# Attention, two mixtures of experts, one core: the second expert of the first mixture joins the block-by-block part

## The chip, the cores and the metric

One core of one Trainium2 chip runs the whole program. The metric is device time in microseconds (us). TensorE is PE in the profile, VectorE DVE, ScalarE ACT, GpSimd POOL, and SyncE SP; SP issues nearly all the transfers. PEld is TensorE's loading of weights.

## The reference

```
q, k, v: 2 batches x 8 heads x 768 tokens x 64
scores = q k^T / 8 - slope(h) * distance; kept: keys 0..7 and the last 96 keys
a = softmax(scores);  x = a v, as 1536 tokens x 512
mixture 1 (4 experts, all of them for every token):
    y = sum over e of p[:, e] * (relu(x @ w1[e]) @ w2[e]),   w1: 512 x 1024, w2: 1024 x 512
mixture 2 (8 experts, 192 tokens each, chosen by a greedy ranking of y @ w_gate):
    out[tokens of e] = relu(y[tokens of e] @ v1[e]) @ v2[e]
```

## The kernel before

**Numbers in two halves.** Each float32 operand of a matmul is scaled by a power of two and split into two float16 halves, hi and lo, and each product is three matmuls (hi hi, hi lo, lo hi). A weight matrix is fetched in two raw halves of 1 MB (`w_load`, L372); `w_norm` takes its sum of squares on ACT (L402) and turns it into a scale; then hi is made on ACT, POOL or DVE (`w_hi`, `scaled_on`, L540 to L544) and lo on DVE (`w_lows`, L473).

**Jobs.** The eight weight matrices of the first mixture are jobs 0 to 7, two for each expert. Job k's halves are `wl0.k` and `wl1.k` in the order below.

**First part (`phase1`).** Tokens come in 12 blocks j of 128. For each block the attention is done (load, scale, split, transposes by DMA, `qk`, `max` L706, `exp` L715, `ph` and `pl` that split the probabilities, `PT`, `pv`, `x`, `xT`: L770 issues the transpose of the finished block), and expert 0 follows behind: `g` (first layer, 12 matmuls of 128 columns per step, L834), `relu`, `hhi`, `hlo`, `y` (second layer, 3 matmuls of 512 columns per step, L845), `add`. Jobs 0 to 3 are fetched and split in between. The program order of all that is written out by hand in `ORDER1`, a list of names with a block number behind the point and an engine behind the slash; where no engine is named, the table `ENGINE` gives it. `AFTER` and the `after=` lists only check the order. Each engine runs its own instructions in this order.

**Second part (in `build`).** Expert 1 goes over the 12 blocks in three groups of four: 96 first-layer matmuls of 512 columns for each group, then 96 second-layer matmuls of 512. Meanwhile `pump` fetches and splits jobs 4, 5 and 6 (L402, L445, L447, L454).

**Third part (`phase3`)** runs experts 2 and 3 in pairs of blocks with the ranking of tokens behind; then `route`, in which the first weights of the second mixture are fetched into five raw buffers; then the second mixture, whose weights go through nine raw buffers.

The rule by which the second part groups its work:

```
jobs = [(e, j) for e in range(1, last - 1) for j in range(0, NB, 4)]
for e, j0 in jobs:
    ...
    for f in range(8):
        ps, st = s.g1(Ws[e], j0, j0 + 4, f, 1)
        ...
        s.hidden(ps, hh[:, f:f + 1], hl[:, f:f + 1])
        s.pump(1)
```

Of the kernel before, what the change touches and what calls it, by code (L numbers as in the profile page):

```python
# [42 lines left out]

ORDER1 = """
    load sq1 sq0 sq2 wl0 run wl1 route total scale wsq0 hi1/V load.1 hi0/A wsq1 lo1 lo0 hi2 sq1.1 lo2 wsum wsc gate0
    whi5 sq0.1 whi1/A whi3/V sq2.1 gate1 whi2/V wlo5 gate2 T0 T1 whi4/A run.1 load.2 total.1 wlo3 whi7/A swap tiles
# [2 lines left out]
    consts swap.1 keys.1/A max3 hi2.2 exp3 wsq0.1 lo2.1 pl0/V kglob.1 lo1.2 hi0.2 pl1/V qk0.1 ph2 load.3 sq1.3 lo0.2
    max0.1 exp0.1 PT0 wlo6 qk1.1 max1.1 pl2 qk2.1 ph3 pl3 PT1 bias1.1 max2.1 qk3.1 sq0.3 max3.1 pv lo2.2 wsq1.1 x  # L50
    ph0.1 pl0.1 wsum.1 sq2.3 T1.2 norm exp1.1 exp2.1 wsc.1 keys.2/G run.3 ph1.1/A both ph2.1/A total.3 T0.2 bias0.2
    whi1.1 rscale scale.3 xhi/V kglob.2 values.1/G load.4 exp3.1 xlo sq1.4 swap.2 xT pl1.1 wlo1.1 PT0.1 hi2.3/V hi1.3
    qk0.2 max0.2 lo1.3 pl2.1 ph3.1/A whi5.1/A pl3.1 qk1.2 sq0.4 lo2.3 wlo4 whi2.1 hi0.3/A vglob.1 g00 pe0 sq2.4
    bias1.2/A exp0.2 max1.2 g01 whi4.1 lo0.3 g02 g03 PT1.1 g10 T1.3 run.4 ph0.2 total.4 T0.3 wlo2.1 g11 qk2.2 pv.1
    scale.4 whi7.1 max2.2 qk3.2 load.5 x.1 swap.3 exp1.2 exp2.2 hi1.4 hi0.4 relu0 keys.3 bias0.3 pl0.2/V max3.2 norm.1
    g12 ph1.2/A ph2.2/V hhi0/A rscale.1 g13 xhi.1 exp3.2 sq1.5 whi3.1 lo0.4 kglob.3 xlo.1 pl2.2 whi0.1 ph3.2 wlo5.1
    sq0.5 lo1.4 T0.4 pl1.2/V qk0.3 xT.1 pl3.2 qk1.3 sq2.5 max0.3 max1.3 relu1 T1.4 qk2.3 values.2 qk3.3 hi2.4/A g00.1
    g01.1 g02.1 wlo0.1 vglob.2 bias1.3/A wlo4.1 PT0.2 keys.4 hhi1/A PT1.2 exp0.3 bias0.4 exp1.3 g03.1 whi6.1 ph0.3/A
    g10.1 run.5 hlo0 swap.4 max2.3 total.5 scale.5 y00 g11.1 y01 hi1.5 pv.2 g12.1 pl0.3/V ph1.3/A hi0.5 hlo1/V lo2.4
    kglob.4 lo0.5 pl1.3/V relu0.1 wl0.2 exp2.3 y02 x.2 qk0.4 g13.1 max3.3 norm.2 bias1.4 ph2.3/V wlo3.1 rscale.2  # L60
    exp3.3 load.6 xhi.2 PT0.3 sq1.6 hi2.5/V max0.4 xlo.2 qk1.4 ph3.3 lo1.5 wlo6.1 y03 T0.5 xT.2 exp0.4 sq0.6 pl2.3
    sq2.6 y04 max1.4 y05 qk2.4 pl3.3 T1.5 max2.4 qk3.4 values.3/G exp1.4 ph0.4 y06 exp2.4 run.6 keys.5 total.6 vglob.3
    wlo7.1 max3.4 kglob.5 g00.2 bias0.5 g01.2 scale.6 y07 tiles.1 relu1.1/V ph1.4 pl0.4/V pl1.4 g02.2 hi1.6 hhi0.1/A
    swap.5 g03.2 pe0.1 exp3.4 PT1.3 hlo0.1 qk0.5 lo2.5 pv.3 g10.2 hi0.6/A x.3 g11.2 ph2.4/A pl2.4 g12.2 load.7 max0.5
    y00.1 lo0.6 ph3.4/V sq1.7 PT0.4 bias1.5 norm.3 T0.6 rscale.3 qk1.5 pl3.4/V bias0.6 xhi.3/G hhi1.1 exp0.5 max1.5
    hlo1.1 PT1.4 sq0.7 values.4/A sq2.7 g13.2 qk2.5 ph0.5 xlo.3 add0 vglob.4 max2.5 y01.1 lo1.6 y02.1 hi2.6/V run.7
    pe0.2 xT.3 y03.1 y04.1 pl0.5 qk3.5 y05.1 exp1.5 relu0.2/V y06.1 ph1.5 exp2.5 lo2.6 max3.5 swap.6 pv.4 T1.6 y07.1
    ph2.5/A g00.3 total.7 g01.3 x.4 g02.3 pl1.5 relu1.2 scale.7 tiles.2 exp3.5 ph3.5/A hhi0.2 hi1.7/V bias1.6 qk0.6
    pl2.5 g03.3 norm.4 hi0.7/A pl3.5 PT0.5 qk1.6 hlo0.2 rscale.4 g10.3 max0.6 load.8 xhi.4/V hi2.7 g11.3 g12.3 g13.3
    values.5/A y00.2 sq1.8 lo0.7 qk2.6 hhi1.2/A xlo.4 PT1.5 lo1.7 exp0.6 y01.2 relu0.3/V y02.2 sq0.8 max1.6 pe0.3  # L70
    y03.2 T0.7 bias0.7 hlo1.2 ph0.6 y04.2 xT.4 T1.7 sq2.8 y05.2 qk3.6 vglob.5 y06.2 exp1.6 pv.5 y07.2 ph1.6 tiles.3
    max2.6 exp2.6 run.8 lo2.7 keys.7/G relu1.3/V pl0.6/V hhi0.3 load.9 hlo0.3 g00.4 add0.1/V kglob.7 g01.4 g02.4 g03.4
    total.8 g10.4 y00.3 swap.7 hhi1.3/G relu0.4 hlo1.3 g11.4 max3.6 x.5 exp3.6 y01.3 norm.5 ph2.6/V y02.3 pl2.6
    ph3.6/A sq1.9 scale.8 hi1.8 g12.4 qk0.7 y03.3 sq0.9 hi0.8/V qk1.7 pl1.6 y04.3 pl3.6/V lo0.8 rscale.5 xhi.5 bias1.7
    max0.7 g13.4 sq2.9 xlo.5 wl1.2 PT0.6 bias0.8 hi2.8/V max1.7 lo1.8 qk2.7 PT1.6 pe0.4 y05.3 T0.8 xT.5 y06.3 exp0.7
    y07.3 tiles.4 ph0.7 exp1.7 hhi0.4/G qk3.7 hlo0.4 max2.7 pv.6 T1.8 add0.3/V exp2.7 ph1.7 swap.8 add0.2 relu1.4
    lo2.8 y00.4 load.10 max3.7 y01.4 x.6 ph2.7 y02.4 keys.8/A g00.5 g01.5 run.9 exp3.7 y03.4 pl2.7/V total.9 kglob.8
    ph3.7/A g02.5 pl0.7 scale.9 qk0.8 g03.5 max0.8 norm.6 qk1.8 pl1.7 hhi1.4/A rscale.6 sq1.10 PT0.7 bias1.8 pl3.7
    exp0.8 g10.5 hlo1.4 g11.5 hi1.9 values.7 hi0.9/V pe0.5 g12.5 ph0.8 y04.4 lo0.9 qk2.8 g13.5 vglob.7 bias0.9/A
    max1.8 y05.4 sq0.10 y06.4 lo1.9 xhi.6/V relu0.5/V hi2.9/A qk3.8 PT1.7 xlo.6 pl0.8 y07.4 tiles.5 sq2.10 T0.9 exp1.8  # L80
    hhi0.5/G hlo0.5/V pv.7 relu1.5 T1.9 y00.5 keys.9/A max2.8 y01.5 ph1.8 xT.6 exp2.8 run.10 y02.5 hhi1.5/G lo2.9
    hlo1.5 pl1.8 max3.8 y03.5 exp3.8 swap.9 x.7 norm.7 load.11 total.10 y04.5 PT0.8 y05.5 g00.6 ph2.8 ph3.8/A kglob.9
    pl2.8 scale.10 rscale.7 g01.6 y06.5 xhi.7/G qk0.9 pl3.8/V hi1.10/A g02.6 g03.6 max0.9 sq1.11 xlo.7 qk1.9 hi0.10/A
    y07.5 sq0.11 exp0.9 PT1.8 relu0.6/V max1.9 g10.6 tiles.6 hhi0.6/A bias1.9 pe0.6 qk2.9 exp1.9 values.8 xT.7
    bias0.10 lo0.10 g11.6 g12.6 g13.6 hlo0.6 add0.4 ph0.9/V T0.10 vglob.8 qk3.9 sq2.11 max2.9 lo1.10 y00.6 y01.6 pv.8
    g00.7 T1.10 relu1.6 g01.7 exp2.9 run.11 pl0.9 max3.9 hhi1.6/A g02.7 g03.7 swap.10 values.9 keys.10 x.8 exp3.9
    ph1.9 y02.6 pl1.9 ph2.9 kglob.10 total.11 g10.7 hlo1.6 PT0.9 g11.7 g12.7 scale.11 ph3.9/A norm.8 qk0.10 qk1.10
    y03.6 hi2.10/A rscale.8 pl2.9 g13.7 max0.10 pl3.9 qk2.10 hi1.11/A PT1.9 xhi.8 relu0.7 exp0.10 xlo.8 xT.8 bias1.10
    ph0.10 y04.6 y05.6 max1.10 vglob.9 max2.10 y06.6 hi0.11/V hi2.11/V exp1.10 y07.6 pv.9 exp2.10 ph1.10 lo0.11 qk3.10
    tiles.7 hhi0.7 T0.11 max3.10 g00.8 g01.8 relu1.7 lo2.10 lo2.11 lo1.11 pl0.10 ph2.10/A hlo0.7/V pe0.7 values.10/G  # L90
    g02.8 exp3.10 g03.8 hhi1.7 add0.6 g10.8 pl2.10 x.9 add0.5/V T1.11 ph3.10/V g11.8 relu0.8/V g12.8 y00.7 y01.7
    pl1.10 y02.7 hlo1.7 swap.11 close0 keys.11 bias0.11/A y03.7 kglob.11 gate3 y04.7 wsq0.2 y05.7 pe0.8 y06.7 norm.9
    y07.7 qk0.11 rscale.9 PT0.10 wsq1.2 qk1.11 g13.8 max0.11 tiles.8 hhi0.8/A pl3.10 relu1.8/V hlo0.8 max1.11 y00.8
    y01.8 vglob.10 qk2.11 PT1.10 xhi.9 xlo.9 y02.8 bias1.11 y03.8 pv.10 exp0.11 qk3.11 hhi1.8 max2.11 wsum.2 hlo1.8/V
    ph0.11/A exp1.11 y04.8 exp2.11 pl0.11/V ph1.11 max3.11 xT.9 y05.8 ph2.11/V pl1.11/V y06.8 pl2.11/V y07.8 g00.9
    g01.9 x.10 exp3.11 ph3.11/A pl3.11/V norm.10 tiles.9 add0.7/V g02.9 g03.9 g10.9 g11.9 g12.9 relu0.9/V PT0.11
    rscale.10 hhi0.9/G hlo0.9/V pe0.9 g13.9 xhi.10/G y00.9 relu1.9/V values.11/A xlo.10 vglob.11 hhi1.9 wsc.2 y01.9
# [1748 lines left out]
```

## Time and profile before

| | |
|---|---|
| median of 3 runs | 895.22 us (891.95 to 895.56) |
| the profiled execution | 895.84 us, of which the span of its instructions is 894.1 us |
| busy over the span | PE 755.8 us (85%), DVE 645.1 (72%), PEld 544.6 (61%), ACT 528.1 (59%), POOL 334.4 (37%) |
| mean granted TensorE clock | 0.962 of 2.4 GHz |

PE's busy time counts each matmul to its modelled end, and matmuls overlap, so what a stretch of matmuls costs is read from start to start. DVE's instructions overlap a little as well: the sum of their durations is larger than the time in which DVE was busy.

### The profile page before, as it was taken

To read this page: it belongs to the slowest core of one execution; us is meant where nothing else is said; L and a number is where in the kernel's file an instruction comes from. 1 tells how busy PE (TensorE), PEld (TensorE's weight loads), DVE (VectorE), ACT (ScalarE), POOL (GpSimd) and SP (SyncE) were. 2 spreads that over 40 slices of the span, in tenths; PEclk is the share of its full clock that TensorE was granted. 3 is DMA by queue.
4 is the path that set the end of the run, shared out by engine and by line. 5 is a ranking of instruction groups with operands and counts; after the bars stand their busy time and mean duration, and the time that the engine had idled before them with its cause. 6 is when DMAs were issued, how large, how long until landed. Compare 5 with 4: busy or idle time off the path is not lost.

```text
span 894.1 us, 19304 instructions
## 1 busy us (share of the span) xinstructions
PE 755.8 (85%) x7539; PEld 544.6 (61%) x7539; DVE 645.1 (72%) x1710; ACT 528.1 (59%) x1046; POOL 334.4 (37%) x403
## 2 busy tenths in 40 slices
...
GB/s 232 217 177 184 178 188 212 151 112 139 154 142 0 108 81 1 95 31 89 1 26 12 14 25 14 36 2 1 59 213 84 131 139 347 247 277 321 193 34 39
DMA packets 196860, 105.20 MB, mean 118 GB/s; under 512 B 167585, under 2 KB 167585, under 8 KB 196769
## 3 DMA queue, kind: packets, MB, share of 16 engines
...
## 4 chain that ended last, share of the span: by engine, by line
PE 41%; DVE 25%; issue 12%; DMA 9%; ACT 7%; POOL 4%; SPq 1%; POOLq 0%; DVEq 0%; ACTq 0%
PE pH L834 16%; PE pY L845 14%; DVE C L967 3%; PE pR L834 2%; PE pY L1012 2%; ACT junk L402 2%; DVE jk L970 2%; DMA xt<-xs 2%; DVE t L706 2%; DMA xk<-in_k_dram 2%; PE pH L1255 2%; DMA xg<-g 2%; DVE w L473 1%; PE pR L1275 1%; POOL out_dram L1291 1%
## 5 line engine op out<-in xcount | busy, mean ns | idle before, releaser
L834 PE MATMUL pH<-xT,w 128*128 128x128 f16 (+2 forms) x2304 | 238.7, 263 | 10.7 <-DMA xT<-xs 9.2
L834 PEld LDWEIGHTS <-w 128*128 128x128 f16 x2592 | 209.0, 100 | 61.8 <-DMA xT<-xs 7.1
L845 PE MATMUL pY<-w,hh 128*128 128x512 f16 x544 | 162.3, 380 | 3.7 <-DVE y L544 1.3
L808 ACT ACTIVATE H<-pH 128x512 f32<-128x512 f32 (+1 forms) x94 | 52.8, 564 | 100.6 <-PE pH L834 75.8
L845 PE MATMUL pY<-w,hl 128*128 128x512 f16 x272 | 103.4, 380 | 4.2 <-POOL hl L1383 3.1
L980 ACT ACTIVATE Cj<-C 128x128 bf16<-128x128 bf16 (+11 forms) x88 | 75.3, 856 | 43.1 <-DVE C L967 42.1
L542 POOL TENSOR_SCALAR hh<-H 128x512 f16<-128x512 f32 x55 | 36.6, 665 | 134.3 <-ACT H L808 123.8
L845 PEld LDWEIGHTS <-hh 128*128 128x128 f16 x544 | 49.9, 98 | 52.9 <-issue 2.6
L1255 PEld LDWEIGHTS <-w 128*128 128x128 f16 x768 | 65.5, 100 | 23.4 <-DMA xg<-g 18.5
L432 DVE SCALAR_TENSOR_TENSOR w<-raw,wsr,w 128x1024 f16<-128x1024 f32 x52 | 65.2, 1278 | 6.3 <-ACT w L540 6.3
L1275 PE MATMUL pR<-hh,w 128*128 128x192 f16 x512 | 67.1, 249 | 0.0
L1255 PE MATMUL pH<-xg,w 128*128 128x192 f16 x528 | 49.8, 254 | 20.2 <-DMA xg<-g 18.3
L803 DVE TENSOR_TENSOR hl<-H,hh 128x384 f16<-128x384 f32 (+1 forms) x56 | 34.6, 617 | 44.2 <-POOL hh L542 43.1
L967 DVE TENSOR_SCALAR C<-LR,Lg 128x1024 bf16<-128x1024 f32 (+7 forms) x88 | 64.1, 729 | 3.1 <-PE pw L986 1.7
L1275 PEld LDWEIGHTS <-w 128*128 128x128 f16 x768 | 64.7, 99 | 2.3 <-issue 2.0
L1275 PE MATMUL pR<-hl,w 128*128 128x192 f16 x256 | 63.8, 249 | 0.0
L1012 PE MATMUL pY<-w,xT 128*128 128x512 f16 x192 | 61.6, 396 | 0.0
L402 ACT ACTIVATE w<-raw 128x2048 f16<-128x2048 f32 x18 | 34.3, 1905 | 42.1 <-PE pY L845 23.4
L715 ACT ACTIVATE t<-t,mx,ec 128x256 f32<-128x256 f32 (+1 forms) x96 | 55.2, 576 | 2.9
L540 ACT ACTIVATE w<-raw,wsr 128x1024 f16<-128x1024 f32 (+1 forms) x49 | 50.7, 1053 | 6.5 <-DVE wsr L302 6.5
L852 DVE SCALAR_TENSOR_TENSOR y<-pY,pe,y 128x512 f32<-128x512 f32 x22 | 16.5, 748 | 51.6 <-PE pY L845 47.0
L695 PE MATMUL pS<-kT,qT 128*128 128x128 f16 x176 | 29.4, 245 | 25.9 <-DVE mx L706 9.9
...
## 6 DMA issues: line engine op xcount, KB each, us to landing
...
pt<-pp SPq DMA_TRANSPOSE x24, 4.9
```

The source lines that it names most:

```text
L402: A.activation(x, s.raws[k, q][0], AF.Square, accum_out=J["ss"][:, q:q + 1])
L432: V.scalar_tensor_tensor(l, r[:, d2], sc, h, op0=OP.mult, op1=OP.subtract)
L540: s.nc.scalar.activation(out, x, AF.Copy, scale=sc)
L715: s.nc.scalar.activation(t[:, o + hh], t[:, o + hh], AF.Exp, bias=mx[:, 1, hh:hh + 1], scale=e[:, 0:1], accum_out=s.SU[j][:, 2 * g + hh:2 ...
L808: s.nc.scalar.activation(H, ps, AF.Relu, scale=HS)
L834: nc.tensor.matmul(o[f], w[:, d, 128 * (f0 + f):128 * (f0 + f) + 128], x[:, :, c], start=(d == 0 and i == 0), stop=(d == 3 and i == 2))
L845: nc.tensor.matmul(py, l[:, f], w[:, f], start=(f == 0 and i == 0), stop=(f == 7 and i == 2))
L967: V.tensor_scalar(C[:, 8 * i:8 * i + n], x[:, :n, e], l, None, op0=OP.is_ge)
L980: s.nc.scalar.activation(x, C, AF.Copy, accum_out=s.AC[j][:, 1, e:e + 1])
L1012: nc.tensor.matmul(py, a[:, f], w[:, f], start=(n == 0), stop=(n == 23))
L1255: nc.tensor.matmul(ps[0][:, f % 2], w[:, d, 128 * f:128 * f + 128], xg[:, :, c], start=(k == 0), stop=(k == 11))
L1275: nc.tensor.matmul(ps[0][:, d % 2], w[:, f, 128 * d:128 * d + 128], h[:, f], start=(k == 0), stop=(k == 23))
```

## The change

Expert 1 is taken out of `build` and put into `phase1`, two blocks behind expert 0 (`LAG = 2`), with names in capitals (`G`, `Relu`, `Hhi`, `Hlo`, `Y`, `Add`). Its first layer is now done in steps of 128 columns, as expert 0's. Its weights get a place of their own (`wa`; expert 0's and later expert 3's are in `wc`). Raw halves of jobs 0 to 3 are fetched into parts of `y` and `xT` that are not in use yet, those of jobs 4 to 7 into `hl3`, which is opened when attention's memory is free (`close1`). Jobs 4, 5 and 6 are fetched and split in the order too, after `close1`, and half 1 of job 7 is fetched at its end. `w_hi` and `w_lows` take 1024 elements at a time and not 512. The bias of the scores is made for two heads at a time and its instructions are spread over three engines (`bias0` to `bias3`); q, k and v share five buffers. `ORDER1` is written anew, with other engines for many steps. In `phase3` three buffers and not four hold the transposed weights for the gate. In `route` the five raw buffers are two in `wc`, two in `wb[0]` that are used once, and one new one; two more in `wc` come back for the second mixture.

```
-ENGINE = dict(whi="G", hi="G", bias="G", keys="V", values="V", ph="G", pl="G", xhi="A", relu="A", hhi="V",
-              hlo="G", add="A")
+ENGINE = dict(whi="A", hi="A", bias="A", keys="V", values="V", ph="V", pl="V", xhi="A", relu="A", hhi="A",
+              hlo="V", add="A", Relu="A", Hhi="A", Hlo="V")
...
+LAG = 2
...
 ORDER1 = """
+    load gate0 loadv gate1 gate2 sq1 sq0 wl0 sq2 wsq0 run wl1 total scale wsq1 wl0.1 wl1.1 wsum load.1 hi1/V bias0/G
+    lo1 loadv.1 wsq0.1 hi2/G hi0/V lo2 lo0 wsc wsq1.1 whi1/V whi2/V whi3 bias1/G sq1.1 wsum.1 wlo2 sq0.1 wlo1 wsc.1
+    sq2.1 T0 T1 whi0/G wlo0 wlo3 run.1 whi1.1/V whi3.1 whi0.1 wl0.2 swap total.1 bias2/G wl1.2 scale.1 qk0 hi1.1/G
...
+    vglob.11 Y6.6 PT1.11 Y7.6 G03.7 pv.11 Tiles.7 G10.7 xT.10 x.11 hhi1.8/G close1 norm.11 Add.6 Relu0.7 G11.7 wl0.4
+    rscale.11 xhi.11 G12.7 wl1.4 xlo.11 wsq0.4 xT.11 pe.8 add.7/V G13.7 y0.8 wsq1.4 Pe.7 y1.8 y2.8 g00.9 hlo1.8/G
...
+    G12.11 G13.11 Y4.10 Relu1.11 Hhi0.11/V Y5.10 Y6.10 Y7.10 whi3.6/G Hlo0.11 Hhi1.11/G Add.10 Y0.11 Y1.11 Y2.11
+    Hlo1.11/G Y3.11 Y4.11 wlo3.6 Y5.11 Y6.11 Y7.11 Add.11 wl1.7
 """.split()
...
+    def place(s, m, e, i):
+        if (m, e) == (1, 1) or m == 2 and e % 2 == 0:
+            if i == 0 and e < 2:
+                s.wA = s.wa.tile([128, 2, 2, 4096], F16, name="w")
+            return s.wA[:, i]
+        p = s.wc if m == 1 and e != 2 else s.wb[i]
+        return p.tile([128, 2, 4096], F16, name=f"w{i}")
...
+        f, d = divmod(c, 2)
         J = s.WJ[k]
+        d = slice(2 * d, 2 * d + 2)
         s.scaled_on(eng, J["parts"][f][0][:, d], s.raws[k, f][0][:, d], J["sc"])
...
+        slots = [lambda: s.y[:, 4:8], lambda: s.y[:, 8:12], lambda: early(4), lambda: early(8)] * 2 + \
+            [lambda: hid3(4), lambda: hid3(8), lambda: hid3(0)] * 3
+        for k in range(8):
...
+        while n2 < NB:
+            e = 0 if n1 < NB and n1 - n2 < LAG else 1
+            j = (n1, n2)[e]
...
             s.phase1(inner, scores, big, pool, re)
-            W = s.finish(1, 1)
...
-            jobs = [(e, j) for e in range(1, last - 1) for j in range(0, NB, 4)]
-            prev, adds = None, []
...
-                prev = (e, j0, hh, hl, pe)
-            second(prev)
...
             W = s.finish(1, last - 1)
-            w1 = s.finish(1, last, 0)
...
-            raw = pool(top, "raw", 5, side="right", **re)
-            s.rawfree = [raw] * 5
+            raw = pool(top, "raw", 1, **right, **re)
...
+            s.rawfree = two(s.wc, 0) + [tuple(x) for x in two(s.wb[0], 0)] + [raw]
...
-            s.rawfree += [raw2] * 4
+            s.rawfree += [raw2] * 4 + two(s.wc, 1)
```

## Rows read from the trace of the kernel before

**Rows 1.** Busy time by stretches, with granted clock, DMA share and GB/s

```profile
0.00:50.00 50.00, 8.89 (x80) 6.90 (x80) 39.95 (x149) 36.57 (x88) 20.91 (x31) 1.00 1.04 221
50.00:234.60 184.60, 156.49 (x2124) 121.30 (x2124) 176.18 (x477) 133.47 (x348) 122.74 (x127) 0.96 0.85 157
256.30:380.70 124.40, 124.40 (x581) 56.44 (x580) 48.16 (x76) 31.38 (x47) 32.35 (x42) 1.00 0.24 68
380.70:894.10 513.40, 450.77 (x4624) 349.02 (x4622) 372.31 (x993) 318.70 (x553) 154.12 (x199) 0.95 0.37 102
...
50.00:110.00 60.00, 43.23 (x592) 36.88 (x592) 56.62 (x152) 46.19 (x125) 41.46 (x43) 0.89 0.94 177
```

**Rows 2.** Chain that ended last: start, length, what

```profile
234.60 6.45 DMA xT<-xs
...
256.46 15.54 PE pH L834 x72
...
380.86 5.24 PE pH L834 x48
```

**Rows 3.** Transposes of finished blocks, issued by SP: first and last start

```profile
L770 SPq DMA_TRANSPOSE xT<-xs x12: 1232/1294/2117, 50.0 to 234.6; - x12
```

**Rows 4.** PE in order of time: start, duration, matmuls of one kind

```profile
209.60 1.56 PE L753 MATMUL pO<-vs,pt 128*128 128x64 f16 x48
...
226.00 5.52 PE L834 MATMUL pH<-xT,w 128*128 128x128 f16 x96
231.36 0.59 PE L845 MATMUL pY<-w,hh 128*128 128x512 f16 x2
...
297.79 0.59 PE L845 MATMUL pY<-w,hh 128*128 128x512 f16 x2
...
298.44 0.59 PE L845 MATMUL pY<-w,hh 128*128 128x512 f16 x2
```

**Rows 5.** DVE by line and shape, 0 to 256 us: count, busy us, mean ns

```profile
L473 DVE SCALAR_TENSOR_TENSOR w<-raw,wsr,w 128x512 f16<-128x512 f32 x21 | 17.3, 851 | 0.8 <-POOL w L542 0.8
...
L730 DVE TENSOR_TENSOR pp<-t,pp 128x512 f16<-128x512 f32 x12 | 9.0, 755 | 0.0
...
L1383 DVE TENSOR_TENSOR hl<-H,hh 128x512 f16<-128x512 f32 x7 | 5.4, 776 | 1.0 <-POOL hh L542 0.9
...
L818 DVE SCALAR_TENSOR_TENSOR pe<-p,wboth,tsc 128x1 f32<-128x1 f32 x12 | 4.7, 391 | 0.0
...
L544 DVE TENSOR_SCALAR pp<-t 128x512 f16<-128x512 f32 x6 | 3.0, 500 | 0.0
```

**Rows 6.** DVE, the same view from 380 us on

```profile
L432 DVE SCALAR_TENSOR_TENSOR w<-raw,wsr,w 128x1024 f16<-128x1024 f32 x52 | 65.2, 1278 | 6.3 <-ACT w L540 6.3
...
L544 DVE TENSOR_SCALAR w<-raw,wsr 128x1024 f16<-128x1024 f32 x13 | 10.0, 770 | 0.0
```

**Rows 7.** DVE, the same view, 256 to 384 us

```profile
L852 DVE SCALAR_TENSOR_TENSOR y<-pY,pe,y 128x512 f32<-128x512 f32 x12 | 9.0, 750 | 33.2 <-PE pY L845 28.7 <-PE pw L408 4.4
```

**Rows 8.** SP in order of time: fetches of raw weights in the first part

```profile
2.88 1.50 SPq L372 DMA_DIRECT2D raw<-in_moe_w_dram  x2
...
27.55 0.65 SPq L372 DMA_DIRECT2D y<-in_moe_w_dram  x1
...
79.35 1.99 SPq L372 DMA_DIRECT2D raw<-in_moe_w_dram  x1
...
235.90 4.00 SPq L372 DMA_DIRECT2D raw<-in_moe_w_dram  x3
```

**Rows 9.** Who waited for whom, 45 to 240 us: total, times, longest

```profile
PE pS L695 <- DVE mx L706: 9.3, 4, 5.1
```

**Rows 10.** SP in order of time: fetches for the second mixture

```profile
641.92 6.02 SPq L372 DMA_DIRECT2D raw<-in_moe_w_dram  x5
...
721.44 0.38 SPq L372 DMA_DIRECT2D raw<-in_moe_w_dram  x1
```

**Rows 11.** Who waited for whom, 738 to 850 us

```profile
ACT junk L402 <- DMA raw<-in_moe_w_dram: 1.6, 2, 1.1
```

More of the change, by code (lines that the diff above doesn't have):

```diff
@@ L49 @@
[L49 to L97, printed above, removed]
-    y02.9 PT1.11 hlo1.9 y03.9 whi2.2 pv.11 y04.9 whi7.2/V y05.9 whi6.2 whi0.2/A whi1.2 y06.9 xT.10 whi3.2/A whi5.2
@@ new lines @@
+    T1.1 ph0 lo2.1 qk2 pl0 qk3 max2 wlo0.1 bias0.1/G swap.1 keys.1/G exp1 max3 kglob.1 loadv.2 wsum.2 ph1/G consts
+    wl0.3 wsc.2 sq1.2 bias1.1/G qk0.1 exp2 whi3.2/V max0.1 exp3 pl1 qk1.1 qk2.1 sq0.2 ph2/G sq2.2 ph3/G run.2 pl2
+    pl3/G max1.1 total.2 qk3.1 whi1.2 wl1.3 bias2.1/G scale.2 bias3.1/G PT0 hi1.2/G hi0.2/V PT1 exp0.1 max2.1 hi2.2/G
+    lo0.2 load.3 T0.2 pv wsq0.3 lo2.2 lo1.2 x T1.2 wsq1.3 exp1.1 norm loadv.3 ph0.1/G sq1.3 exp2.1 wsum.3 swap.2 wsc.3
+    tiles bias0.2/G load.4 pl0.1/G max3.1 sq0.3 keys.2 rscale wlo1.2 gate3 both ph1.1/A bias1.2/G xhi/G kglob.2 xlo
@@ new lines @@
+    qk0.2 pl1.1/G sq2.3 run.3 max0.2 ph2.1/G total.3 qk1.2 pl2.1 xT exp3.1 ph3.1/G exp0.2 qk2.2 pl3.1/G g00 scale.3 pe
+    g01 g02 hi1.3 hi2.3/G max1.2 bias2.2 hi0.3/G values.1 lo0.3 exp1.2 tiles.1 whi0.2/V bias3.2 lo1.3 vglob.1 PT0.1
+    PT1.1 g03 ph0.2/G T0.3 qk3.2 max2.2 relu0 g10 loadv.4 max3.2 hhi0/G pv.1 g11 hlo0 T1.3 y0 y1 x.1 g12 sq1.4 ph1.2/A
+    exp2.2 g13 norm.1 pl0.2/G bias0.3/V ph2.2/A rscale.1 xhi.1/V xlo.1 sq0.4 keys.3 y2 swap.3 xT.1 sq2.4 pl1.2/G
+    bias1.3/G run.4 kglob.3 lo2.3 relu1 total.4 pl2.2 y3 values.2/A exp3.2 qk0.3 load.5 PT0.2 max0.3 whi0.3/G qk1.3
@@ new lines @@
+    ph3.3/G xhi.2 hi0.5 bias1.4 pl2.3 pl3.3/G y3.1 Relu0 xlo.2 y4.1 sq1.6 PT0.3 vglob.3 y5.1 PT1.3 lo1.5 Hhi0 max0.4
+    G13 hi2.5/G xT.2 bias2.4 whi3.3 qk1.4 y6.1 qk2.4 Relu1 add y7.1 wlo1.3 pv.3 g00.2 sq0.6 loadv.6 lo0.5 max1.4 g01.2
+    max2.4 g02.2 g03.2 qk3.4 sq2.6 x.3 Hlo0/G g10.2 T0.5 Hhi1/G norm.3 lo2.5 add.1 rscale.3 bias3.4/G tiles.2 T1.5
+    run.6 xhi.3 relu0.2 swap.5 hhi0.2 wlo0.3 keys.5/A xlo.3 bias0.5/V load.7 Hlo1/G g11.2 whi2.3/G total.6 xT.3 g12.2
+    kglob.5 hlo0.2/G g13.2 scale.6 Pe exp0.4 wlo2.3 ph0.4/G pl0.4/G Y0 max3.4 G00.1 qk0.5 Y1 G01.1 exp1.4 hi1.6 G02.1
```

373 lines of the change are left out of this document (202 added, 171 removed).

## Prediction

> **What bounds the kernel now.** I read the busy time by stretches first, then the chain that ended last, then PE and SP in order of time, and DVE by line and shape. The reader is to see three stretches that hang on different engines. From 50 to 234.6 us, while attention runs, DVE is busy 176.2 of 184.6 us, 95%, and the first and last `xT` are issued at 50.0 and 234.6 [rows 1, 3]. So attention goes at DVE's pace. From 256.3 to 380.7, expert 1, PE is busy all of 124.4 us and DVE only 48.2, ACT 31.4, POOL 32.4 [rows 1]; the chain there is PE from 256.46 to the first matmuls of the third part at 380.86, and before it lies a 6.45 us wait for the transpose of the last block [rows 2]. The remaining 513 us hang on other work [rows 1], which the change reaches only through buffers. The two stretches are complementary: one leaves PE room, the other leaves DVE, ACT and POOL room. The change lays them over each other, so the question is when the third part begins: 380.9 us before, T after.
>
> **PE's work.** First-layer matmuls of 128 columns: 96 from 226.00 to 231.36, so 55.8 ns each, 0.67 us for a step of 12 [rows 4]. Those of 512 columns: 72 in 15.54 us, 216 ns each [rows 2]; four times 55.8 is 223, so expert 1's first layer in smaller pieces costs 288 x 7 ns = 2 us more. A second-layer step is three matmuls, 297.79 to 298.44, 0.65 us [rows 4]. An expert costs 8 x 0.67 + 8 x 0.65 = 10.6 us for a block, 127 for twelve. Attention's own matmuls: 352 for the scores at 56 ns, 20 us, and eleven times the 1.56 us of a 48-group for the values, 17 us [rows 4]. In all 2 x 127 + 37 = 291 us of PE, which the old kernel needs 381 us to get through.
>
> Counting names in the new order, 135 `g` and `G` steps and 120 `y` and `Y` steps stand before `xT.11`: 135 x 0.67 + 120 x 0.65 + 37 = 205 us of PE. Behind it stand 57 and 72: 38 + 47 = 85 us.
>
> Here a rule speaks against the change. The Trainium skill, "TensorE: Matmul & The Clock Gate", section "Back-to-back issue gap", says that in a real stream of weight loads and matmuls the spacing is about 81 ns at 128 columns and 131 ns at 512, since each weight load takes its share; by it the first layer of expert 1 would go from 288 x 131 = 38 us to 1152 x 81 = 93 us, an estimate of 55 us lost. The trace disagrees at both sizes, 55.8 and 216 ns in runs of 96 and 72 with a weight load for each, so the sum goes by the rows.
>
> **DVE's work before `xT.11`**, old order against new, priced from the shapes' own means [rows 5 to 7]. `hlo` and `Hlo` on DVE 5 to 16 names: 11 x 0.776 = +8.5 us. `Add` +7 x 0.750 = +5.3; `add` on DVE 5 to 2, -2.2 at the same price. `bias` on DVE 0 to 11: no row shows it there; the nearest, as many elements at 500 ns (`pp`), gives +5.5, and the ends are 0 (it saves POOL and ACT the same) and 11 x 0.78 = 8.6. `ph` +7 x 0.5 = +3.5; `pl` +3 x 0.755 = +2.3; `pe`, `Pe` +4 x 0.391 = +1.6. Hi and lo of weights: lo was 24 x 0.851 = 20.4 and is 16 x 1.278 = 20.4; hi on DVE is 5 of 1024 elements at 0.770 for 3 of 512 at about 0.6, +2. `hi`, `keys`, `values` on DVE are 7 fewer at about 0.65, -4.5; `xhi` 2 more, +1.3; `relu`, `hhi` and scales +1.5, the smaller first-block bias -1. Sum +23.8 of durations; DVE's instructions overlap a little, so I take 22. At DVE's pace attention ends at 234.6 + 22 = 257 us.
>
> **Where the two meet.** In the new order more weight work stands ahead of `xT.0`: nine lo's of 1024 (11.5 us) where seven of 512 stood (6 us), two more scales, a `max` and two hi's more on DVE; I take 8 us, so it comes at 58 and not at 50. PE has some 5 us behind it by then and must do 200 more before `xT.11`: 258 us if it never waited. So both engines are full at once, which the old kernel never asks. From `xT.0` to `xT.11` its PE did 88 x 0.67 + 80 x 0.65 + 37 - 5 = 143 us in 184.6, 77%, without being the engine that set the pace. The ends are therefore 258 (PE full) and 58 + 200/0.77 = 318 (PE no fuller than before). The nearest row for an engine that does set the pace is DVE in that very stretch, 95% full [rows 1]; I take that for PE: 58 + 200/0.954 = 268.
>
> Behind `xT.11` PE has 85 us, and no transpose to wait for, as the last block is needed only after 33 steps of the first and 37 of the second layer, 46 us: the 6.45 us go. That tail now hides the splitting of jobs 4 to 6, which expert 1 hid before: some 42 us of DVE (12 lo's at 1.278 among them), 24 of ACT and 25 of POOL, each well under 85; without that cover DVE's part would show in full. I add 2 us for `relu` queued on ACT behind a sum of squares. 268 + 85 + 2 = 355.
>
> **Transfers.** Before, five raw halves were fetched by 80 us and the rest at 134 and later, the last three at 235.90 [rows 8]. The new order fetches four ahead of block 1's q and k, and all eight ahead of `xT.0`: 3 MB more there, on SP's one queue, ahead of the `T`, `PT` and loads of blocks 1 to 4. At the 177 to 221 GB/s of these stretches, with a DMA share of 0.94 and 1.04 [rows 1], that is 14 to 17 us of transfer. The ends are 0, if DVE splits weights meanwhile, and 16; I take 3, since the order holds such work ready. T = 358. The fetches behind `close1` go ahead of `xT.11` on SP, 2 MB, some 8 us, and the last block has the 46 us above as cover.
>
> **Later parts.** Three buffers for the transposed gate weights and the moved ranking tiles I cost at nothing: `start` and the gate come a whole pair of blocks before the first use; uncovered it would be one transpose, 1.3 us to issue [rows 3]. In `route` two of five raw buffers are used once, so seven halves of the second mixture are fetched before it starts and not nine (five at 641.92, the last of four more at 721.44 [rows 10]). The missing 2 MB follow at once when it starts. ACT waited for raw weights only 1.6 us there [rows 11], so the ends are 0 and some 8 us; I take 1.
>
> **Sum.** The profiled execution takes 895.84 us, 0.6 above the median of 895.22. 895.84 - (380.9 - 358) + 1 = 873.9; I say 874.
>
> **Rivals.** *Transfers first* (0.16): early blocks wait for the 3 MB, 13 us more than I took, T = 371, total 887. For it: DMA share 1.04 at the start. Against: much of DVE's first 60 us is then weight work.
>
> *PE in front of DVE* (0.15, the other side): expert 1's steps stand in PE's one queue ahead of `qk`, and DVE's `max` waits for them. The old kernel shows the waits only the other way round, PE's scores on DVE, 9.3 us [rows 9]. Net, 205 - 148 = 57 us of PE are added ahead of `xT.11`, where 148 is the old 88 and 80 steps plus 37. If all showed, attention would end at 257 + 57 = 314, T = 404, total 920. It becomes slower than before when more than about 37 of the 57 show (end of attention at 294). Middle: 902.
>
> *Better overlap* (0.08): PE nearly never waits, T = 258 + 85 = 343, total 859.
>
> *Weight loads that show*, by the rule above (0.02): if half of the 56 ns were added to each of expert 1's 1152 short matmuls, 32 us, T = 390, total 906; against it stand the 96 in a row.
>
> Forecast (0.59): 874, own range 863 to 885.
>
> **Numbers.** 0.5% is 4.5 us, about what a measurement of this kernel can tell from no change. Faster by more: the forecast, better overlap, two thirds of transfers first, 0.78. Within: the rest of transfers first and a little of PE in front, 0.08. Slower: 0.14. The range 857 to 894 leaves out most of PE in front of DVE, the weight loads and the edges of the rest, some 0.2.
>
> **What would show it.** In the changed profile: `xT.11` near 268, the first matmuls of 256 columns near 358, PE's steps still at 56 ns, DVE around 90% busy until then, and no group of 128x512 first-layer matmuls. If `xT.0` comes after 65, transfers were first. If PE waits little but DVE falls under 80% between 60 and 260, PE stands in front. Wrong altogether would be a third part or a second mixture that grows by more than 5 us, since I took both as they are.

## The result, and the profile after

The changed kernel takes 886.2 us (median of 9 runs, 883.7 to 890.72) where the kernel before takes 894.86 (9 runs, 889.18 to 896.72): a ratio of 0.9919, 95% interval 0.9891 to 0.9947. It is faster, by 8.7 us, about 1%. The forecast was 874, some 21 us faster. The profiled execution took 887.16 us, with a span of 885.4; against the 895.84 of the execution before that is 8.7 as well, so the traces can be compared directly.

Busy time by stretches, in the same form as [rows 1]. The first four rows are cut at `xT.0`, `xT.11` and the start of the third part; the rows behind the first "..." cut the second of them, and the last two are pieces of the third.

```profile
0.00:59.00 59.00, 9.30 (x81) 7.01 (x81) 48.09 (x154) 43.71 (x92) 25.18 (x36) 1.00 1.03 250
59.00:275.60 216.60, 207.40 (x2814) 162.49 (x2815) 179.21 (x510) 150.35 (x376) 97.47 (x96) 1.00 0.71 130
275.60:370.10 94.50, 86.97 (x889) 60.64 (x888) 38.52 (x60) 29.33 (x39) 22.72 (x20) 0.96 0.28 88
370.10:885.40 515.30, 447.91 (x4623) 348.07 (x4621) 369.63 (x993) 314.03 (x548) 153.99 (x199) 0.96 0.39 105
...
59.00:110.00 51.00, 42.75 (x607) 35.65 (x608) 47.30 (x129) 39.75 (x94) 28.57 (x27) 1.00 0.89 158
110.00:174.00 64.00, 63.88 (x868) 49.86 (x866) 57.37 (x175) 51.60 (x138) 32.60 (x34) 1.00 0.76 139
174.00:234.60 60.60, 59.77 (x766) 45.06 (x764) 52.69 (x150) 38.91 (x96) 24.70 (x25) 1.00 0.65 126
234.60:275.60 41.00, 41.00 (x585) 31.91 (x583) 21.85 (x59) 20.09 (x50) 11.60 (x11) 1.00 0.50 88
...
275.60:290.00 14.40, 12.24 (x119) 8.65 (x118) 2.76 (x9) 5.90 (x8) 2.92 (x3) 0.88 0.66 185
345.00:352.00 7.00, 7.00 (x62) 5.04 (x61) 6.76 (x11) 0.63 (x1) 2.78 (x3) 0.76 0.00 0
```

From 110 us on PE is busy for all of each stretch while DVE falls from 90% to 53%: attention, which hung on DVE before, now hangs on PE. Only in the ramp, 59 to 110, is it DVE (93%) with PE waiting. The third part begins at 370.1 instead of 380.9, and from there on 515.3 us follow instead of 513.2 (894.1 - 380.9).

The transposes of finished blocks, as in [rows 3]:

```profile
L807 SPq DMA_TRANSPOSE xT<-xs x12: 1232/1256/2000, 59.0 to 275.6; - x12
```

The chain that ended last, as in [rows 2]:

```profile
255.22 1.40 PE pO L790 x48
256.62 4.02 PE pH L871 x72
...
272.28 8.79 DMA hl<-in_moe_w_dram
281.09 2.01 ACT w L432 x2
...
298.55 2.40 DVE w L515 x2
300.97 5.22 DMA hl<-in_moe_w_dram
306.22 2.01 ACT w L432 x2
...
330.62 2.40 DVE w L515 x2
333.49 8.78 DMA hl<-in_moe_w_dram
342.29 2.01 ACT w L432 x2
...
362.32 7.77 PE pY L882 x36
370.09 5.24 PE pH L871 x48
```

Two things are read here. PE's prices stand: 72 first-layer matmuls in 4.02 us are 55.8 ns each and 36 second-layer ones in 7.77 us are 216 ns, as before. And three times, from 272 us on, the chain leaves PE: a raw half of a weight matrix lands in `hl3` (DMA), ACT takes its sum of squares (L432), and PE goes on. Twice the fetch itself had to wait until DVE had made the lo's of an older half (L515), since its buffer is one of three.

PE's own timeline behind `xT.11`: the three rows with idle time in front, and what follows the first and the third (start, duration, matmuls; the bracket is idle time and what ended it).

```profile
283.96 1.25 PE L871 MATMUL pH<-xT,w 128*128 128x128 f16 x12 [2.16 <-ACT H L845]
...
285.07 1.44 PE L871 MATMUL pH<-xT,w 128*128 128x128 f16 x12
...
287.58 0.85 PE L871 MATMUL pH<-xT,w 128*128 128x128 f16 x12
...
308.60 0.16 PE L438 MATMUL pq<-wsb,ones 128*128 128x1 bf16 x1 [1.76 <-ACT wsb L435]
...
344.68 0.16 PE L438 MATMUL pq<-wsb,ones 128*128 128x1 bf16 x1 [3.60 <-ACT wsb L435]
```

The waits are 2.16 + 1.76 + 3.60 = 7.5 us. The first is a `relu` on ACT behind a sum of squares; the other two are single one-column matmuls, the sum of a weight's squares over the partitions (`wsum`), that stand in PE's one queue and hold up everything behind them. And 12 matmuls took 1.25 and 1.44 us after the first wait, where a later such row has 0.85; from 285.07 to the next matmul at 286.30 they cost 102 ns each, nearly twice 55.8, and the granted clock from 285.0 to 287.6 is 0.50, the lower of its two levels, 1.2 GHz. The stretches above with granted clocks of 0.88 and 0.76 lie around the first wait and right behind the third. Together they cost 14.4 x 0.12 + 7 x 0.24 = 3.4 us.

ACT's timeline at the same places, each sum of squares with its wait for the transfer:

```profile
276.98 1.91 ACT L432 ACTIVATE w<-hl 128x2048 f16<-128x2048 f32 x1 [2.21 <-DMA hl<-in_moe_w_dram]
281.09 1.91 ACT L432 ACTIVATE w<-hl 128x2048 f16<-128x2048 f32 x1 [2.11 <-DMA hl<-in_moe_w_dram]
283.33 0.58 ACT L845 ACTIVATE H<-pH 128x512 f32<-128x512 f32 x1
...
306.22 1.91 ACT L432 ACTIVATE w<-hl 128x2048 f16<-128x2048 f32 x1 [3.27 <-DMA hl<-in_moe_w_dram]
...
338.13 1.91 ACT L432 ACTIVATE w<-hl 128x2048 f16<-128x2048 f32 x1 [5.68 <-DMA hl<-in_moe_w_dram]
342.29 1.91 ACT L432 ACTIVATE w<-hl 128x2048 f16<-128x2048 f32 x1 [1.68 <-DMA hl<-in_moe_w_dram]
```

ACT is busy 31% of this stretch. It is not short of time; it stands still, with the `relu` at 283.33 queued behind it.

PE in the ramp, 59 to 110 us, by line and shape (count, busy us, mean ns, idle before):

```profile
L871 PE MATMUL pH<-xT,w 128*128 128x128 f16 x325 | 22.4, 233 | 1.8 <-DMA xT<-xs 1.8
L882 PE MATMUL pY<-w,hh 128*128 128x512 f16 x32 | 9.5, 379 | 0.0
L736 PE MATMUL pS<-kT,qT 128*128 128x128 f16 x44 | 7.2, 247 | 1.3 <-DMA qT<-qT 1.3
L735 PE MATMUL pS<-kT,qT 128*128 128x128 f16 x43 | 7.1, 246 | 0.9 <-DVE mx L745 0.9
L882 PE MATMUL pY<-w,hl 128*128 128x512 f16 x16 | 6.1, 379 | 0.0
L790 PE MATMUL pO<-vs,pt 128*128 128x64 f16 x144 | 4.9, 193 | 1.8 <-DMA pt<-pp 1.8
```

A busy PE is not a full one, so count: 325 x 55.8 ns + 48 x 216 + 87 x 56 + 144 x 29 (128 x 64: 48 in 1.40 us in the chain above) = 18.1 + 10.4 + 4.9 + 4.2 = 37.6 us of work in 51, 74%. The same count for the later three windows gives 63.8 of 64, 59.9 of 60.6 and 41.3 of 41.

Who waits for whom has turned round. Before, PE's scores waited for DVE, 9.3 us [rows 9]; after, from 59 to 275 us:

```profile
DVE xo L802 <- PE pO L790: 14.8, 5, 4.9
...
DVE t L745 <- PE pS L736: 2.8, 5, 1.1
```

### The profile page after: what moved, and what is told of

Its sections match the earlier page's. It is cut to its first block, busy times and chain, and to the rows that moved or that the text cites. A ratio compares the mean times of both kernels' runs of the same rounds, so it can differ in the third digit from the quotient of the medians.

```text
span 885.4 us, 20978 instructions
## 1 busy us (share of the span) xinstructions
PE 751.6 (85%) x8403; PEld 578.2 (65%) x8403; DVE 635.5 (72%) x1714; ACT 537.4 (61%) x1054; POOL 299.4 (34%) x350
## 4 chain that ended last, share of the span: by engine, by line
PE 41%; DVE 21%; issue 12%; DMA 12%; ACT 9%; POOL 3%; SPq 1%; POOLq 0%; ACTq 0%; DVEq 0%
PE pH L871 17%; PE pY L882 13%; DVE C L1004 3%; ACT junk L432 3%; DMA hl<-in_moe_w_dram 3%; PE pR L871 2%; PE pY L1049 2%; DVE jk L1007 2%; DMA y<-in_moe_w_dram 2%; DVE w L515 2%; DMA pt<-pp 1%; DMA w<-in_moe_w_dram 1%; ACT w L580 1%; PE pO L790 1%; POOL out_dram L1328 1%
## 5 line engine op out<-in xcount | busy, mean ns | idle before, releaser
L871 PEld LDWEIGHTS <-w 128*128 128x128 f16 x3456 | 250.1, 99 | 38.8 <-issue 7.1
L871 PE MATMUL pH<-xT,w 128*128 128x128 f16 (+1 forms) x3168 | 251.2, 236 | 3.9 <-ACT H L845 2.2
L882 PE MATMUL pY<-w,hl 128*128 128x512 f16 x272 | 103.5, 381 | 0.0
L1292 PEld LDWEIGHTS <-w 128*128 128x128 f16 x768 | 66.5, 101 | 31.5 <-DMA xg<-g 18.4
L1004 DVE TENSOR_SCALAR C<-w,Lg 128x1024 bf16<-128x1024 f32 (+7 forms) x112 | 74.5, 682 | 3.7 <-PE pw L1023 1.8
L1312 PEld LDWEIGHTS <-w 128*128 128x128 f16 x768 | 63.4, 98 | 4.6 <-issue 4.5
L582 POOL TENSOR_SCALAR hh<-H 128x512 f16<-128x512 f32 x40 | 27.3, 682 | 108.8 <-ACT H L845 76.7
L1049 PE MATMUL pY<-w,xT 128*128 128x512 f16 x192 | 59.7, 385 | 0.0
L1432 POOL TENSOR_TENSOR hl<-H,hh 128x512 f16<-128x512 f32 x25 | 33.4, 1337 | 50.1 <-ACT hh L580 41.1
L584 DVE TENSOR_SCALAR hh<-H 128x384 f16<-128x384 f32 (+1 forms) x43 | 16.6, 387 | 46.0 <-ACT H L845 40.8
L882 PEld LDWEIGHTS <-hl 128*128 128x128 f16 x272 | 26.7, 98 | 32.5 <-issue 0.6
L768 POOL TENSOR_TENSOR pp<-t,pp 128x512 f16<-128x512 f32 (+1 forms) x29 | 34.8, 1203 | 31.8 <-DVE pp L584 17.0
L1049 PE MATMUL pY<-w,hl 128*128 128x512 f16 x112 | 44.3, 395 | 0.0
L1007 DVE SCALAR_TENSOR_TENSOR jk<-w,Lg,notbefore 128x128 bf16<-128x128 f32 x96 | 42.6, 444 | 0.0
```

The costliest lines, as they stand in the source:

```text
L768: (G if eng == "G" else V).tensor_sub(pl[:, x], t, ph[:, x])
L871: nc.tensor.matmul(o[f], w[:, d, 128 * (f0 + f):128 * (f0 + f) + 128], x[:, :, c], start=(d == 0 and i == 0), stop=(d == 3 and i == 2))
L882: nc.tensor.matmul(py, l[:, f], w[:, f], start=(f == 0 and i == 0), stop=(f == 7 and i == 2))
L1004: V.tensor_scalar(C[:, 8 * i:8 * i + n], x[:, :n, e], l, None, op0=OP.is_ge)
L1007: V.scalar_tensor_tensor(jk, s.LRof[j][:, e], l, s.notbefore, op0=OP.is_equal, op1=OP.mult, accum_out=s.AC[j][:, 0, e:e + 1])
L1049: nc.tensor.matmul(py, a[:, f], w[:, f], start=(n == 0), stop=(n == 23))
```

## The experiments

The theory: PE is full from 110 us on, so between there and the third part each microsecond that PE waits is lost; behind `xT.11` it waits 7.5 us for weights that are not there and loses more to the clock. Rivals: transfers pace the start and everything after is shifted; DVE still sets the pace, through larger weight splits or later transposes. Ten kernels tell these apart. Times are medians in us; `xT.0`, `xT.11` and T (the first 128x256 matmuls of the third part) are from each kernel's profile (first starts; the chain counts T 0.2 us later); the ratio is to the kernel before, run on the same chip.

| kernel | median | ratio, 95% | xT.0 | xT.11 | T |
|---|---|---|---|---|---|
| before | 894.86 | | 50.0 | 234.6 | 380.7 |
| after | 886.2 | 0.9919 (0.9891 to 0.9947) | 59.0 | 275.6 | 369.9 |
| tail_order | 878.02 | 0.9816 (0.9781 to 0.9851) | 58.9 | 277.2 | 360.8 |
| tail_both | 876.62 | 0.9817 (0.9781 to 0.9853) | 56.7 | 274.7 | 357.8 |
| third_e1 | 852.84 | 0.9538 (0.9488 to 0.9589) | 58.7 | 261.8 | 335.7 |
| no_lo_e1 | 883.23 | 0.9871 (0.9828 to 0.9914) | 56.9 | 273.1 | 365.9 |
| early_order | 880.84 | 0.9859 (0.983 to 0.9887) | 61.2 | 276.6 | 362.5 |
| no_xlo | 876.92 | 0.9815 (0.9786 to 0.9845) | 59.2 | 273.8 | 359.5 |
| split512 | 880.55 | 0.9838 (0.981 to 0.9867) | 61.2 | 277.5 | 364.0 |
| no_fetch_e1 | 876.11 | 0.9792 (0.9761 to 0.9823) | 56.9 | 274.6 | 359.4 |
| hi_pool | 877.35 | 0.9813 (0.978 to 0.9846) | 58.5 | 276.7 | 363.5 |
| before_early4 | 903.43 | 1.0101 (1.0063 to 1.0138) | 59.7 | 243.8 | 390.1 |

One profile stands behind each `xT` and T. The kernels after, tail_order, tail_both and no_xlo issue the same steps up to `xT.3`, and yet their profiles have `xT.0` at 56.7 to 59.2 and `xT.3` at 112.0 to 114.6. So 2.6 us at these points, and what T inherits of it, is scatter and no effect of an edit.

**tail_order.** The changed kernel with parts of the scales of jobs 4 to 6 moved back in the order: job 4's sums of squares (`wsq`) go behind the `relu` that they held up, the one-column matmuls (`wsum`) of jobs 4 to 6 go some steps later, and job 6's `wsc` and three of its hi's follow.

```diff
 ORDER1 (each name goes to just before another one)
-g10.9 wsum.4 Hhi1.7      -wsq0.4 xT.11      -y0.8 wsq1.4 Pe.7
+g10.9 wsq0.4 Hhi1.7      +wsq1.4 y7.8       +wsum.4 Y0.7
-y7.9 wsum.5 Hhi1.8/V     -wsq1.6 wsum.6 wl0.7 wsc.6 y0.11
+wsum.5 Y2.8              +wsum.6 wsc.6 y1.11
 whi2.6 whi1.6 whi0.6 to before y2.11
```

> The changed kernel with nothing but the order of its tail altered: the sums of squares of job 4 behind the relu of block 7, and the one-column matmuls that add up jobs 4, 5 and 6 some steps later. Theory (PE stands in its tail because these matmuls and one relu sit behind ACT, which waits for raw weights; 7.5 us of waits and some 4 us of lowered clock): most of the waits go, the third part starts 5 to 8 us earlier than the 370.1 us of the changed kernel, the whole takes 878 to 882. Rival (PE's tail is full work, the waits only move to the next place): no gain, 885 to 888.

Its windows, cut at its own `xT.0`, `xT.11` and T:

```profile
58.90:277.20 218.30, 209.28 (x2814) 164.01 (x2815) 177.66 (x511) 150.92 (x376) 98.13 (x96) 0.98 0.72 129
277.20:360.80 83.60, 83.44 (x888) 58.29 (x887) 39.98 (x61) 28.64 (x38) 22.71 (x20) 1.00 0.32 99
```

The tail takes 83.6 us instead of 94.5, PE is busy in all of it and the clock is 1.00: not one wait is left, and the clock's loss went with the waits. ACT still stands before sums of squares until their transfers land, 3.60 us at 304.25 and 5.61 at 334.12, much as before; PE is no longer held up by it. T is 9.2 us earlier, more than expected, and the time 8.2 us shorter. Attention itself (218.3) is no faster, so the whole gain is from the tail.

**tail_both.** tail_order, and the raw halves behind attention go round four buffers instead of three.

```diff
-[hid3(4), hid3(8), hid3(0)] * 3
+[hid3(0), s.rx.tile([128, 4, 512], F32, name="raw"), hid3(4), hid3(8)] * 2
```

> The same order as tail_order and a fourth raw buffer of 1 MB in the tail, so that job 5 is fetched whole without waiting for job 4's split. Theory: the two late sums of squares no longer wait for transfers (3.3 and 5.7 us of ACT's waits), 1 to 3 us beyond tail_order, 876 to 880. Rival (once the order is mended the fetches are covered): the same as tail_order.

The tail is 357.8 - 274.7 = 83.1 us, 0.5 less than with three buffers, and the median 876.62 against 878.02 with overlapping ranges (875.4 to 882.08, 876.07 to 879.02). T is 3.0 us earlier, but 2.2 us of that are there at `xT.0` already, where the two kernels do not differ. Three buffers are enough in this order; a fourth in the old order of the tail was not tried.

**third_e1.** The changed kernel with only the first of the three products of expert 1 in both layers; hi lo and lo hi are left out, two thirds of 127 us, 84 us of PE.

```diff
-for i, (w, c) in enumerate(((W[0], d), (W[0], 4 + d), (W[1], d))):
+p = ((W[0], d), (W[0], 4 + d), (W[1], d))[:1 if thin else 3]
+for i, (w, c) in enumerate(p):
 # the same in g2; thin = (e == 1)
```

> Leaves out two of every three matmuls of expert 1 (the hi-lo and lo-hi products), in the changed kernel: 84 us of PE less, every other instruction as before. Theory (PE sets the pace from 110 us on): attention's last transpose, 275.6 in the changed kernel, comes at about 257 to 260, where DVE's work alone ends, and the third part begins at 310 to 330 and not at 370. Rival (attention is held by DVE and by waits between engines, PE merely looks full): the last transpose stays within 5 us of 275.6 and only the tail shrinks, by 32 us at most.

```profile
58.70:261.80 203.10, 167.79 (x2198) 128.06 (x2199) 178.34 (x510) 150.22 (x375) 95.45 (x95) 0.96 0.77 138
261.80:335.70 73.90, 55.76 (x546) 38.60 (x544) 38.95 (x61) 27.03 (x36) 21.88 (x20) 0.88 0.34 110
```

`xT.11` comes 13.7 us earlier, just short of what was expected, and T 34.2, which misses the expected 310 to 330. Of the 84 us, 52 lie ahead of `xT.11` (504 short matmuls and 112 long ones fewer). So PE's load does hold attention, but 14 us show when 52 are taken away, and not all the 57 that the rival of the prediction put at stake; with PE lightened the stretch is still 203 us, 88% of it DVE. The tail shrinks by 21 us only, since with less to do PE arrives earlier at weights that are not there. Its timeline of PE shows the two `wsum` waits grown from 5.4 to 14.8 us:

```profile
290.84 0.16 PE L438 MATMUL pq<-wsb,ones 128*128 128x1 bf16 x1 [5.06 <-ACT wsb L435]
...
322.47 0.16 PE L438 MATMUL pq<-wsb,ones 128*128 128x1 bf16 x1 [9.78 <-ACT wsb L435]
```

**no_lo_e1.** The changed kernel with expert 1's lo weights set to zero in place of being made: eight instructions of 1024 elements, 1.34 us on the mean, become fills of 0.49 us. One of them stands ahead of `xT.0` in the order, five more ahead of `xT.3` and two behind it.

```diff
+if k in (2, 3):
+    s.nc.vector.memset(J["parts"][f][1][:, d], 0.0)
+    return
```

> Puts zeros where the lo halves of expert 1's weights are made: eight DVE instructions of 1.28 us become short ones, all ahead of the second block, PE unchanged. Theory (up to 110 us DVE sets the pace and PE is only three quarters full, and behind that PE is full): the early transposes come 5 to 8 us earlier, and the third part starts 4 to 8 us earlier. Rival one (transfers pace the start): transposes and total unchanged. Rival two (DVE paces all of attention and PE has room): the last transpose also moves by 8 us, while PE's share falls.

`xT.0` comes 2.1 us earlier, which is within the scatter and misses the 5 to 8 expected; `xT.3` comes 4.6 earlier (110.0 for 114.6, where the unchanged kernels have 112.0 at the earliest), T 4.0, and the median is 3.0 us shorter, with ranges that hardly overlap (880.08 to 884.64 against 883.7 to 890.72). So of some 6.8 us that DVE is given around the ramp, 3 to 4 reach T, as they should where DVE paces.

**no_xlo.** tail_order, with the lo half of the finished block set to zero from block 4 on: eight DVE instructions of 0.91 us become fills of 0.27, some 5 us taken away after about 120 us.

```diff
-at("xlo", j, put, j, s.rows_lo)
+at("xlo", j, put, j, no_lo if j > 3 else s.rows_lo)   # no_lo: memset(xs[:, 512:1024], 0.0)
```

> tail_order with zeros written where the lo half of the finished block is made, for blocks 4 to 11: eight DVE instructions of about 1 us become short ones, all between 120 and 280 us. Theory (PE alone sets the pace from 110 us on): last transpose and third part within 1.5 us of tail_order (277.2 and 360.8), the whole within 2 us of 878. Rival (DVE holds this stretch as much as PE does): both 3 to 6 us earlier.

T moves by 1.3 us and the median by 1.1, with overlapping ranges, as the theory has it. At `xT.11` the theory missed: it comes 3.4 us earlier, so DVE's work has a part in when attention ends. PE is busy all the same from 120 us to there, has the same work to do up to T, and that is what the third part waits for.

**split512.** tail_order, with hi and lo of the weights made in pieces of 512 again, as before the change.

```diff
-d = slice(2 * d, 2 * d + 2)
+for d in (2 * d, 2 * d + 1):   # one instruction of 512 for each, in w_hi and in w_lows
```

> tail_order with the weights split in pieces of 512 elements, as before the change: twice as many instructions for hi and lo, 28 more on DVE at about 0.4 us each, 12 us in all, 16 of them ahead of the last transpose. Theory (DVE paces only the first 110 us, where 9 of them lie): the third part 3 to 5 us later than 360.8. Rival (DVE's pace counts everywhere): 6 us or more later.

2.3 us later at `xT.0`, 0.3 at `xT.11`, 3.3 at T, and 2.5 us more in the median. The profile is that of the slowest of six runs (886.53), so its times count for less than the median. The wider instructions are worth some 2 to 3 us to the change; they do not hide a loss in it.

**early_order.** tail_order with the start rearranged: block 1's q and k are loaded ahead of the fetches of job 1 (expert 0's second layer), and the scales and hi's of job 1 go later.

```diff
-sq2 wsq0 run wl1 total scale wsq1 wl0.1 wl1.1 wsum load.1 hi1/V ...
+sq2 wsq0 run wl1 total scale wsq1 load.1 wsum hi1/V ... T1 wl0.1 wl1.1 wsq0.1 whi0/G ...
```

> The tail of tail_order and another order at the start: k and q of block 1 are fetched ahead of job 1's raw halves, and these come behind the transposes of block 0; the sums of squares and hi's of job 1 follow later. Theory (2 MB ahead of block 1 and of block 0's transposes cost the start several us of the 9 by which the first finished transpose is later than before the change): that transpose comes at 52 to 56 and not at 59, the third part 2 to 5 us before the 360.8 of tail_order, the whole takes 873 to 877. Rival (DVE's and ACT's weight work sets the start, not the transfers): 58 to 60, no gain.

It missed: `xT.0` comes 2.3 us later and the median is 2.8 longer. This order of the early fetches gains nothing. It also moves steps of ACT, PE and DVE, and which of these made it worse stays open.

**no_fetch_e1.** tail_order without the fetch of jobs 2 and 3 (4 MB); expert 1 is computed from raw weights that lie in the buffers already.

```diff
-s.nc.sync.dma_start(r, src.rearrange("(k p) f -> p k f", p=128))
+if k not in (2, 3):
+    s.nc.sync.dma_start(r, src.rearrange("(k p) f -> p k f", p=128))
```

> tail_order without the fetch of expert 1's raw weights (4 MB, all before 45 us); expert 1 is made from what expert 0's fetches left, with the same instructions. Theory (the early 4 MB delay the first blocks, as 4 MB did in the old kernel by 9 us): first finished transpose at 50 to 55 and not 59, the fourth 5 to 9 us earlier than 113.4, the third part 4 to 8 us before 360.8. Rival (weight splitting on DVE and ACT sets the start): within 2 us of tail_order everywhere.

The theory missed. The kernel is 2.0 us earlier at `xT.0`, 2.5 at `xT.3`, 1.4 at T and 1.9 in the median, none of it clear of the scatter. So the early 4 MB cost at most some 2 us here.

**before_early4.** The kernel before, with four fetches of 1 MB of expert 1's weights added among the loads of blocks 1 and 3, and nothing done with them.

```diff
+for a in (4, 8) if j in (1, 3) else ():
+    s.nc.sync.dma_start(r, s.w[1][0][1, :, 512 * (a // 8):512 * (a // 8) + 512]...)   # r: part of xT, as raw
```

> The kernel before the change with 4 MB of raw weights fetched besides, which nothing uses: 2 MB ahead of block 1's loads, 2 MB ahead of block 3's. If transfers pace the start, the first finished transpose (50.0 us) comes 6 to 10 us later and the fourth (110.9) 10 to 16 us later. If DVE's work covers them, under 3 us.

9.8 us later at `xT.0`, 9.6 at `xT.3`, 9.4 at T, and 8.5 more in the median. From 40 to 50 us of this kernel DVE and ACT stand still while the DMA engines are full (the busy times are PE, PEld, DVE, ACT, POOL):

```profile
40.00:50.00 10.00, 3.85 (x31) 3.06 (x31) 2.86 (x14) 1.69 (x5) 1.91 (x3) 1.00 1.16 291
```

The same stretch of the kernel before has DVE at 8.98 and ACT at 9.49. So in the old kernel more transfers at the start do delay everything behind, as the rival that blamed transfers has it. In the changed kernel 4 MB cost 2 us at most. Its engines have weights to split meanwhile, and DVE is busy 48.09 of the first 59 us; that this is why they cost less fits, but no run shows it by itself.

**hi_pool.** tail_order, with four early hi's moved from DVE to POOL (`whi1`, `whi2`, `whi1.1` and `whi3.2`).

```diff
-whi1/V whi2/V ... whi1.1/V ... whi3.2/V
+whi1/G whi2/G ... whi1.1/G ... whi3.2/G
```

> tail_order with four early hi's of weights on POOL and not on DVE (4 x 0.8 us of DVE less before 60 us, 4 x 1.7 us of POOL more). If DVE sets the start, the first transposes come 2 to 3 us earlier and the whole takes about 876; if transfers set it, no gain, and a loss of 1 to 3 us where a lo then waits for POOL.

877.35 against 878.02, `xT.0` at 58.5 for 58.9: no difference in the time, though T stands 2.8 us later in its profile (a run of 880.53). Moving work off the busier engine to POOL brought nothing, which speaks against DVE's load alone setting the start. The chain up to `xT.0` in the changed kernel goes through both, with 8.99 + 8.14 + 3.06 + 7.07 = 27 us of transfers in 59; how the two share the start stays open.

## Why the prediction was right in sign and wrong in size

| term | forecast | measured |
|---|---|---|
| `xT.0` | 58 | 59.0 |
| `xT.0` to `xT.11` | 210 | 216.6 |
| `xT.11` to T | 87 | 94.5 |
| reserve for early transfers | 3 | in the first two |
| third part and later | +1 | +2.1 |
| profiled time | 873.9 | 887.2 |

The gain is 380.9 - 370.1 = 10.8 us at T, less 2.1 behind it, which is the 8.7 measured. The error is 13.3 us, of which, but for rounding, 7.5 lie in the tail, 6.6 in attention, 1.1 behind T and 1 at the start, less the 3 held in reserve.

**The step that failed is the tail.** The prediction said: "That tail now hides the splitting of jobs 4 to 6 ... I add 2 us for `relu` queued on ACT behind a sum of squares." The mechanism named was there, 2.16 us of it. What was missing is that the hidden work hangs together with PE in order: a fetch waits for a buffer of three, ACT for the fetch, a one-column matmul for ACT, and all of PE's matmuls for that one. Comparing 42, 24 and 25 us of other engines' work with 85 tells that there is time enough, and nothing of when each piece is due. The tail lost 94.5 - 83.6 = 10.9 us to it, 7.5 of waits and 3.4 of clock, where 2 were allowed; PE's own work there was 83.6 and not 85, so 7.5 of the error remain. tail_order shows the cause by giving the 10.9 back without any work taken away (T = 360.8, time 878.0, within the forecast's own 863 to 885).

**Where the two engines meet** was mis-sized by less, and its picture was wrong. "95% full" was taken for PE over the whole stretch. The average comes out near: 37.6 + 63.8 + 59.9 + 41.3 = 202.6 us of work in 216.6, 94%. But it is 74% in the ramp and all but 100% from 110 us on. So of the 6.6 us, 2.6 are work (202.6 where I had 200 left at `xT.0`) and 4.0 are idle (14 where 10 were allowed). That the sum of this stretch came so near is in part luck, since the share was borrowed from another engine. The consequence matters more than the number: 5 us less for DVE behind 120 us moved T by 1.3 (no_xlo), 6.8 less around the ramp by 4.0 (no_lo_e1).

**DVE's work** came out at half: busy 48.09 + 179.21 = 227.3 us up to `xT.11` against 216.1 before [rows 1], 11.2 more and not 22. The added pieces cost about what they were priced at or more (lo's 1392 and 1290 ns for 1278, `hlo` 872 for 776). What the sum lacked is that untouched instructions got shorter. Those that split k, by line, count, shortest/median/longest ns; first the kernel before, then after:

```profile
L620 DVE SCALAR_TENSOR_TENSOR kn<-xk,asr,kn x12: 739/1184/1665, 10.0 to 197.9; 128x512 f16<-128x512 f32 x12
```

```profile
L658 DVE SCALAR_TENSOR_TENSOR kn<-x,asr,kn x12: 733/740/1171, 10.2 to 213.7; 128x512 f16<-128x512 f32 x12
```

With those of v and q they are 36 instructions and 9.7 us less, of the 10.8 between 22 and 11.2. Since PE decided, this error cost nothing; had DVE decided, the forecast would have been too late by as much. That attention is still 203 us long in third_e1, with DVE at 91% until 234.6 us and at 66% behind it, is more than DVE's own work needs. Which waits between the engines make up the rest was not tried, and stays open.

**Prices of PE** held, 55.8 and 216 ns; only attention's groups of 48 were priced too high, 1.56 us with the end of the last for 1.40 from start to start, 2 us in all. By the Trainium skill, "TensorE: Matmul & The Clock Gate", section "Back-to-back issue gap" (81 and 131 ns in streams with weight loads), the first-layer step would have become dearer; the 72 in 4.02 us and the 36 in 7.77, with a weight load each, disagree with both figures, and the rival built on it is out.

**The other rivals.** Transfers first: not in this kernel (no_fetch_e1, 2 us; `xT.0` at 59 and not after 65), though true of the old one (before_early4). The reserve of 3 us was about right. PE in front of DVE: true in kind, the waits did turn round, but third_e1 gets 14 us back for 52 taken away, and the prediction needed 37 of 57 for a slower kernel. By the prediction's own sign DVE should have fallen under 80% between 60 and 260 us if PE stood in front; it was 85%, and PE set the pace all the same, so that sign was badly chosen. PE's busy share by stretches, and who waits for whom, told it.

**Later parts** were taken as nearly untouched and were: 515.3 for 513.2 us, 1.1 us more than allowed.
